# Left tiles with two lodgers: 592 columns of a half-kept weight granule stay in SBUF

## The chip, the cores and the metric

The kernel runs on one core of one Trainium2 chip. The metric is the device time of one execution in microseconds. All durations below come from one profiled execution or from the timed runs of the kernel before.

## What is computed

The reference adds three things: the input `x` [1, 2048, 1024], a recurrent attention layer on the layer-normalised `xn`, and a routed feed-forward for two rows. The attention sets the time. It walks over 64 segments of 32 rows; each segment takes an 8-row memory that is the output of the segment before:

```python
mem = mem0
for s in range(64):
    xs = xn[:, 32*s:32*(s+1), :]
    h = jnp.concatenate([mem, xs], axis=1)            # 8 + 32 rows
    q, k, v = h @ Wq, h @ Wk, h @ Wv                  # 32 heads of 128; each weight 1024 x 4096
    p = softmax(where(mask, q @ k.T * scale, -1e9))
    o = (p @ v) @ Wo                                  # 4096 x 1024
    mem = o[:, :8, :]                                 # needed by the next segment
    outs.append(o[:, 8:, :])
out = x + concatenate(outs) + routed(xn)
```

The routed part picks the two rows of `xn` with the largest score, sends them through a gated feed-forward (three weights of 1024 x 3584) and adds the result at those rows.

## The kernel before

**Rows.** Of a segment's 40 rows, the first 8 outputs feed the next segment's memory. A segment's "main" rows are the memory and the first 24 rows of x (`XM` = 24). The last 8 rows of a segment, the "left" rows, wait for nobody, so those of four segments (a group `G` of segments with `j` = 0, 1, 2, 3) are put together into 32 rows, and their projections are computed once per group: V with segment j = 0 of the group itself, Q with j = 1 and K with j = 2 for the next group. The left queries and keys go to DRAM (`ql_d`, from `XBl`, line 672) and come back a segment at a time (`LX`, line 453).

**Weights.** The four weights are cut into 64 granules of 128 x 2048 (512 KB): granules 0 to 47 are Q, K and V in six phases of eight (`PHASES`), granules 48 to 63 the output projection, counted by `w`. 44 granules are resident in SBUF. The rest is streamed again in each segment from a DRAM copy (`wsc`) through five slots named `g`; `fetch` (line 329) issues one transfer on the SP queue when a slot comes free. Granule 11 (`KEPT_WHOLE`) has its columns in PSUM (`KEPT`), and granule 25 (`KEPT_PART`) has columns 1024 to 2047 there; `kept_piece` (line 349) copies them into the granule's slot in each segment. So 18 granules travel whole, and of granule 25 columns 0 to 1023, 256 KB.

**Order.** The order of each engine's instructions is the order in which the program issues them (`tc.manual_schedule()`); waits on data are added between them. Work that belongs beside the matmuls is hung on a place `(p, kc)`, after granule kc of phase p, by `hook`; `todo` carries hooks into the next segment. In a segment: six phases of eight granules (lines 641 to 657), each with four matmuls, one for each quarter of the columns; scores, exponent and `soften` for two halves of the heads (hooks (2, 6) to (5, 0)); `attend(0, 0)` at (5, 4) and `attend(0, 1)` at (5, 6), `attend(1, ...)` at w = 5 and 8; the output projection, which begins at line 692. The result goes through `mem_to_st` into the next segment's `ST`.

**The tiles of the change.**

- `PL` [128, 4, 2, 32]: the left rows' probabilities. `clear_pl` at (1, 0) sets the columns of the segment before to zero on POOL (line 591), `soften` writes this segment's columns (line 560), and DVE transposes the whole (line 563) into `PTl`.
- `OTL` [128, 4, 8, 32], tag "otl": the left rows' attention outputs of one group. `attend` writes block j (line 587, on ACT and DVE). At j = 3 its columns are projected into `WL` (line 700); the projections of some resident granules are carried into the next segment, up to hook (2, 2), and `store_left` follows at (2, 4). At j = 1, blocks 2 and 3, still free, hold `XBl`, the left queries on their way to DRAM (line 669).
- `XL`, tag "xl" [128, 256]: the x of the left rows. It is loaded by four DMAs on POOL (line 289) twice in a group: at j = 0 for the next group, where `norm_left` normalises it and `new_stl` at w = 13 turns it into `STL`; and at j = 3 for this group at (2, 0), where `sum_left` at (5, 3) makes the residual of it, which starts the accumulation in `WL` at w = 1 (line 738).
- Tag "vl" [128, 1024]: the left rows' V (`VL`), from phase 4 of j = 0 to `attend(1, 1)` of j = 3; then `OL`, the left rows' output.

Of the kernel before, what the change touches and what calls it, by code (L numbers as in the profile page):

```python
# [19 lines left out]
KEPT_WHOLE = 11  # L20
KEPT_PART = 25
LEFT_OUT = 35
NEG = -30000.0

PHASES = [(0, 0), (1, 0), (0, 1), (1, 1), (2, 0), (2, 1)]
# [3 lines left out]
def kernel(  # L29
# [16 lines left out]
    nc = tc.nc  # L46
# [61 lines left out]
    def columns(g, s):  # L108
        if s > 0 and g == KEPT_WHOLE:
            return None  # L110
        return slice(0, 1024 if s > 0 and g == KEPT_PART else 2048)

    wsc = {g: dram.tile([P, columns(g, 1).stop - columns(g, 1).start], BF16, name=f"wsc{g}")
           for g in streamed if g != KEPT_WHOLE}
# [15 lines left out]

    XS = const.tile([P, 256], BF16, name="XS")
    XN = const.tile([P, 256], BF16, name="XN")
    PL = const.tile([P, 4, 2, 32], BF16, name="PL")
    CT = const.tile([P, 32], F32, name="CT")
    MASK = CT[:, 0:12].bitcast(BF16)
    NEGR = CT[:, 13:14]
# [10 lines left out]
    ML = BS[:, 448:448 + 2 * NT].rearrange("p (t c) -> p t c", c=2)  # L147
    nc.vector.memset(SPS[:, :, :, :], 0.0)
    nc.vector.memset(XN[:, :], 0.0)
    nc.gpsimd.memset(PL[:, :, :, :], 0.0)  # L150
    nc.vector.memset(NMSK, 0.0)

    hm = resident[-1]
# [128 lines left out]
        PTm = turn(OB)  # L282
        nc.vector.tensor_copy(out=gview(st)[:, :, :, XM:SEG], in_=PTm[:, :, :, XM:SEG])  # L283

    def load_left(G):
        t = one.tile([P, 256], BF16, tag="xl", name="XL")
        o4 = x2[4 * G * SEG:4 * (G + 1) * SEG, :].rearrange("(s r) d -> s r d", s=4)
        for g in range(4):
            nc.gpsimd.dma_start(out=t[32 * g:32 * (g + 1), :], in_=o4[:, XM:SEG, 256 * g:256 * (g + 1)])
        return t  # L290
# [38 lines left out]
            nc.sync.dma_start(out=t[:, c], in_=wsc[g][:, :])  # L329
        queued.append((g, t))  # L330

    def part(t, jq):
        return t[:, 512 * jq:512 * (jq + 1)]


    def keep(g, t):
        for c, K in KEPT_COLS[g].items():
            turned = PTB.rearrange("p (i r) -> p i r", i=4)
            for i in range(4):
                nc.tensor.transpose(out=turned[:, i, :], in_=t[:, 512 * c + P * i:512 * c + P * (i + 1)],  # L340
                                    identity=IDENT[:, :])
# [49 lines left out]
    XL0 = load_left(0)  # L391
    OB = one.tile([P, 256], BF16, tag="bA", name="MEM0")
    nc.vector.memset(OB[:, :], 0.0)
    for g in range(4):
# [100 lines left out]
    for s in range(NSEG):  # L495
# [53 lines left out]
        def soften(half):  # L549
            S8 = SPS.rearrange("p i a k -> p (i a) k")  # L550
            DN = one.tile([P, 8], F32, tag="nm", name="DN")
            nc.vector.tensor_reduce(out=DN[:, :], in_=S8, axis=AX.X, op=ALU.add)
            nc.vector.reciprocal(out=DN[:, :], in_=DN[:, :])
            PT2 = one.tile([P, 2, 4, 64], BF16, tag=("bA", "bE")[half], name="PT2")
            PTm, PTl = PT2[:, 0], PT2[:, 1]
            PM = PTl.rearrange("p i q -> p (i q)").rearrange("p (b k) -> p b k", b=8)
            PLt = PL.rearrange("p i a k -> p (i a) k")
            dnb = DN[:, :].unsqueeze(2)
            nc.vector.tensor_tensor(out=PM, in0=S8[:, :, 0:32], in1=dnb.to_broadcast([P, 8, 32]), op=ALU.mult)
            nc.vector.tensor_tensor(out=PLt[:, :, XL * j:XL * (j + 1)], in0=S8[:, :, 32:NK],  # L560
                                    in1=dnb.to_broadcast([P, 8, XL]), op=ALU.mult)
            nc.vector.transpose(out=PTm.rearrange("p i q -> p (i q)"), in_=PM.rearrange("p b k -> p (b k)"))
            nc.vector.transpose(out=PTl.rearrange("p i q -> p (i q)"), in_=PLt.rearrange("p b k -> p (b k)"))
            PTs[half] = (PTm, PTl)

        def attend(half, ph):
# [15 lines left out]
            for jl in range(2):  # L582
# [3 lines left out]
                h0 = 16 * half + 8 * ph + 4 * jl  # L586
                copy(out=left_out()[:, j, :, h0:h0 + 4].rearrange("p r i -> p i r"), in_=ov[:, :, SEG:NK])  # L587

        def clear_pl():
            jp = (j + 3) % 4  # L590
            nc.gpsimd.memset(PL.rearrange("p i a k -> p (i a) k")[:, :, XL * jp:XL * (jp + 1)], 0.0)

        def get_left():
            nxt["xl"] = load_left(G if j == 3 else G + 1)

        def prep_left():
            if j == 0:
                norm_left(nxt["xl"], G + 1)
            else:
                sum_left(nxt["xl"], G)  # L600

        for at, fn in todo:
            hook(*at, fn)
        todo = []
        hook(1, 0, clear_pl)
        if s > 0:
            for c in (0, 2, 1, 3):
                hook(0, (1, 3, 1, 3)[c], lambda c=c: kept_piece(KEPT_WHOLE, c, (nc.scalar.copy, nc.vector.tensor_copy)[c // 2]))
# [5 lines left out]
        hook(3, 3 if j == 2 or s == 0 else 0, lambda: soften(0))  # L614
        if s + 1 < NSEG:
            hook(2, 0, lambda: load_seg(s + 1))
        if j == 3 or (j == 0 and G + 1 < NT):
            hook(2 if j else 3, 0, get_left)
            hook(5, 3, prep_left)
        hook(4, 6, lambda: scores(1))  # L620
        hook(5, 0, exponent)
# [1 line left out]
        hook(5, 4, lambda: attend(0, 0))  # L623
        hook(5, 6, lambda: attend(0, 1))

        def left_pass(PSl, g, Gv, first_, last_):
            for jq in range(4):
                nc.tensor.matmul(PSl[32 * jq:32 * jq + 32, :], lhsT=STL[:, g % KC, :], rhs=part(Gv, jq),  # L628
                                 start=first_, stop=last_, tile_position=(0, 32 * jq))

        left_before = False
        for p, (mat, half) in enumerate(PHASES):
# [8 lines left out]
            for kc in range(KC):  # L641
                g = 8 * p + kc
                Gv = granule(g)
                for jq in range(4):
                    nc.tensor.matmul(PSm[32 * jq:32 * jq + 32, :], lhsT=ST[:, kc, :], rhs=part(Gv, jq),  # L645
                                     start=(kc == 0), stop=(kc == KC - 1), tile_position=(0, 32 * jq))
# [12 lines left out]
            if mat < 2:  # L659
# [3 lines left out]

                def store_ql(mat=mat, half=half, PSl=PSl):
                    if mat == 0:
                        XBl = left_out()[:, 2:4].rearrange("p s r h -> p (s r h)")
                    else:
                        XBl = one.tile([P, 512], BF16, tag=("bA", "vl" if s == 0 else "kt")[half], name="XBl")[:, :]
                    nc.scalar.copy(out=XBl, in_=PSl[:, :])
                    if s == 0:  # L670
                        hooks[p + 1, 3].insert(0, lambda m=mat, h=half, b=XBl: turn_first(m, h, b))
                    (nc.gpsimd if s == 0 else nc.scalar).dma_start(out=ql_d[left[mat]][2 * half + mat], in_=XBl)
# [20 lines left out]
        if s + 1 < NSEG:  # L693
            norm_seg(s + 1)

        def project(PS, w, Gv, lhs, last):
            for hs in range(2):
                h = 2 * w + hs
                for g in range(4):
                    nc.tensor.matmul(PS[32 * g:32 * g + 32, 0:256], lhsT=lhs(h),  # L700
                                     rhs=Gv[:, D * hs + 256 * g:D * hs + 256 * (g + 1)], start=False,
                                     stop=(last and hs == 1), tile_position=(0, 32 * g), skip_group_check=True)

        def lhs_main(h):
# [11 lines left out]
        final = (carried or late or [None])[-1]  # L716
        behind = []
        for w in range(16):
            if w == 5:
# [6 lines left out]
            project(WO, w, Gv, lhs_main, w == 15)  # L726
            if j == 3:
                if w in home_w:
                    fn = lambda w=w, Gv=Gv: project(WL, w, Gv, lhs_left, w == final)
                    if w in late:  # L730
                        fill.append(fn)
                    else:
                        todo.append((((1, 2), (1, 4), (1, 7), (2, 1), (2, 2))[len(todo)], fn))
                else:
                    behind.append((w, Gv))
                if w == 1:
                    WL = psL.tile([P, 512], F32, tag="accl", name="WL")
                    nc.tensor.matmul(WL[:, 0:256], lhsT=IDENT[:, :], rhs=nxt["xl"][:, :], start=True, stop=False,
                                     skip_group_check=True)
                if w >= 1:  # L740
                    for w_, Gv_ in behind:
                        project(WL, w_, Gv_, lhs_left, False)
                    behind = []
            if w == 9 and s + 1 < NSEG:
                new_lx(s + 1)
            if w == 10 and s + 1 < NSEG:
                nxt["st"] = new_st(s + 1)
            if w == 13 and j == 0 and G + 1 < NT:
# [32 lines left out]
    for at, fn in todo:  # L781
# [116 lines left out]
```

## Time and profile before

| | |
|---|---|
| Timed runs, us | 1988.77, 1984.77, 1990.33; median 1988.77 |
| The profiled execution, us | 1984.53 |
| Its span, us | 1982.9 |
| Busy share of the span: PE, DVE, ACT, POOL | 82%, 45%, 37%, 22% |
| Granted TensorE clock, mean | 0.957 |
| Moved by DMA | 712.42 MB, mean 359 GB/s |
| `g<-wsc` issues of 512 KB / 256 KB | 1134 / 63 |
| ... median time from issue to landing, us | 6.0 / 5.0 |

The span runs from the first to the last instruction. In the rows of groups, the numbers behind the bar are the group's busy time in us and the mean ns of one; in the list of waits they are the total in us, the count and the longest. In the timeline, the columns are start, duration, engine, line, operation, tiles, and in square brackets the idle time before it and what ended it. A stretch of the table by windows has busy us and the number of instructions for each engine, then the granted clock, the mean busy share of the 16 DMA engines (packets in flight can bring it a little over 1) and GB/s.

### The profile page before, as it was taken

To read this page: it belongs to the slowest core of one execution; us is meant where nothing else is said; L and a number is where in the kernel's file an instruction comes from. 1 tells how busy PE (TensorE), PEld (TensorE's weight loads), DVE (VectorE), ACT (ScalarE), POOL (GpSimd) and SP (SyncE) were. 2 spreads that over 40 slices of the span, in tenths; PEclk is the share of its full clock that TensorE was granted. 3 is DMA by queue.
4 is the path that set the end of the run, shared out by engine and by line. 5 is a ranking of instruction groups with operands and counts; after the bars stand their busy time and mean duration, and the time that the engine had idled before them with its cause. 6 is when DMAs were issued, how large, how long until landed. Compare 5 with 4: busy or idle time off the path is not lost. (4 is left out here: it accounts for less than half of the span.)

```text
span 1982.9 us, 82788 instructions
## 1 busy us (share of the span) xinstructions
PE 1630.3 (82%) x36080; PEld 893.2 (45%) x36080; DVE 883.9 (45%) x2848; ACT 733.5 (37%) x1995; POOL 436.4 (22%) x883
## 2 busy tenths in 40 slices
PE   3468898989888888989888888989888898988863
PEld 1224444444454444445454444545444444544443
DVE  5834444444444434444454444444444444444430
ACT  1124343434334343433444344443434343343330
POOL 3112213112221311222121221222131122212110
PEclk8669999999999999999999999999999999999995
DMA  9999999999999999999999999999999999999998
GB/s 370 403 340 371 353 358 347 366 362 348 375 336 367 366 336 357 360 367 346 372 356 364 356 360 372 350 371 364 361 355 350 355 362 362 333 369 354 353 391 333
DMA packets 232123, 712.42 MB, mean 359 GB/s; under 512 B 39296, under 2 KB 53168, under 8 KB 231760
## 3 DMA queue, kind: packets, MB, share of 16 engines
q1 hardware_dynamic: 194384, 671.18, 90.9%
q0 software_dynamic: 28736, 28.09, 4.4%
q10 hardware_dynamic: 8640, 7.87, 1.2%
q8 instruction: 282, 4.62, 0.9%
q14 instruction: 81, 0.66, 0.1%
HBM read 694.32 MB, written 22.29 MB: 361 GB/s over the span
## 5 line engine op out<-in xcount | busy, mean ns | idle before, releaser
L645 PE MATMUL PSm<-wres,ST 128*32 128x512 bf16 x8448 | 719.3, 386 | 10.7 <-DVE ST L283 5.4
L645 PEld LDWEIGHTS <-ST 128*32 128x32 bf16 x12288 | 327.0, 96 | 439.2 <-issue 219.6
L645 PE MATMUL PSm<-g,ST 128*32 128x512 bf16 x3840 | 392.4, 388 | 125.6 <-DMA g<-wsc 116.0
L700 PE MATMUL WO<-wres,OT 128*32 128x256 bf16 x5632 | 234.2, 280 | 21.4 <-DMA wres<-in_A_Wo_dram 11.4
L700 PEld LDWEIGHTS <-OT 128*32 128x32 bf16 x8192 | 203.9, 98 | 105.5 <-issue 82.3
L661 ACT CAST XB<-PSm 128x512 bf16<-128x512 f32 x256 | 150.5, 588 | 264.1 <-PE PSm L645 264.0
L453 POOL DMA_DIRECT2D LX<-ql_d x63 | 33.6, 534 | 954.4 <-DVE OTL L587 371.7
L628 PE MATMUL PSl<-wres,STL 128*32 128x512 bf16 x2112 | 201.4, 390 | 5.6 <-ACT VL L688 3.7
L349 DVE COPY g<-KEPT 128x512 bf16<-128x512 bf16 x252 | 95.1, 419 | 195.4 <-PE PSm L645 146.1
L763 POOL DMA_DIRECT2D out_dram<-XN x256 | 129.4, 513 | 226.7 <-DVE XN L761 220.9
L253 POOL DMA_DIRECT2D XN<-in_A_x_dram x256 | 128.8, 508 | 205.1 <-PE PSm L645 69.1
L520 DVE COPY KT<-BT 128x512 bf16<-128x512 bf16 x128 | 53.4, 417 | 245.8 <-PE BT L510 203.3
L700 PE MATMUL WO<-g,OT 128*32 128x256 bf16 x2560 | 133.0, 282 | 34.2 <-DMA g<-wsc 23.2
L684 ACT CAST VM<-PSm 128x512 bf16<-128x512 f32 x128 | 79.5, 621 | 107.3 <-PE PSm L645 107.3
L510 PE MATMUL BT<-IDENT,XB 128*128 128x128 bf16 x1024 | 102.3, 223 | 15.9 <-ACT XB L661 14.5
L510 PEld LDWEIGHTS <-XB 128*128 128x128 bf16 x1024 | 58.7, 98 | 121.9 <-ACT XB L661 71.2
L628 PEld LDWEIGHTS <-STL 128*32 128x32 bf16 x3072 | 83.8, 98 | 65.8 <-issue 15.9
L537 DVE TENSOR_TENSOR BS<-BS,CT 128x96 f32<-128x96 f32 (+1 forms) x256 | 59.7, 233 | 106.8 <-PE BS L530 102.3
L515 ACT COPY QT<-BT 128x512 bf16<-128x512 bf16 x128 | 75.2, 588 | 84.0 <-PE BT L510 43.8
L761 DVE CAST XN<-WO 128x128 bf16<-128x128 f32 x64 | 18.7, 292 | 196.0 <-ACT XN L760 196.0
L578 PEld LDWEIGHTS <-VM 32*128 32x128 bf16 x2048 | 69.7, 91 | 75.7 <-issue 71.5
L547 ACT ACTIVATE BS<-BS 128x320 f32<-128x320 f32 x128 | 54.1, 423 | 119.6 <-DVE BS L543 119.5
(161 smaller groups left out, 2413.8 us busy)
## 6 DMA issues: line engine op xcount, KB each, us to landing
g<-wsc SPq DMA_DIRECT2D x1134, 512.0 KB, 6.0
g<-wsc SPq DMA_DIRECT2D x63, 256.0 KB, 5.0
LX<-ql_d POOLq DMA_DIRECT2D x63, 128.0 KB, 6.1
MW<-in_B_w_gate_dram SPq DMA_DIRECT2D x16, 448.0 KB, 9.5
MW<-in_B_w_up_dram SPq DMA_DIRECT2D x16, 448.0 KB, 9.0
wres<-in_A_Wq_dram SPq DMA_DIRECT2D x12, 512.0 KB, 11.5
MW<-in_B_w_down_dram SPq DMA_DIRECT2D x12, 512.0 KB, 10.1
wres<-in_A_Wk_dram SPq DMA_DIRECT2D x11, 512.0 KB, 13.1
```

The lines of the kernel that those rows point to most:

```text
L253: nc.gpsimd.dma_start(out=XN[32 * g:32 * g + XM, :], in_=x2[s * SEG:s * SEG + XM, 256 * g:256 * (g + 1)])
L349: copy(out=t[:, 512 * c:512 * (c + 1)], in_=KEPT_COLS[g][c])
L510: nc.tensor.transpose(out=PTq[:, il, :, :].rearrange("p j r -> p (j r)"), in_=XB[:, il * P:(il + 1) * P], identity=IDENT[:, :])
L515: nc.scalar.copy(out=QT[half][:, :, :], in_=pv)
L537: nc.vector.tensor_tensor(out=S4, in0=S4, in1=m, op=ALU.add)
L578: nc.tensor.matmul(o, lhsT=VM[half][q0:q0 + 32, il * P:(il + 1) * P], rhs=PTm[q0:q0 + 32, il, 0:NK], start=True, stop=False, tile_position ...
L628: nc.tensor.matmul(PSl[32 * jq:32 * jq + 32, :], lhsT=STL[:, g % KC, :], rhs=part(Gv, jq), start=first_, stop=last_, tile_position=(0, 32 ...
L645: nc.tensor.matmul(PSm[32 * jq:32 * jq + 32, :], lhsT=ST[:, kc, :], rhs=part(Gv, jq), start=(kc == 0), stop=(kc == KC - 1), tile_position= ...
L661: nc.scalar.copy(out=XB[:, :], in_=PSm[:, :])
L684: nc.scalar.copy(out=VM[half][:, :], in_=PSm[:, :])
L700: nc.tensor.matmul(PS[32 * g:32 * g + 32, 0:256], lhsT=lhs(h), rhs=Gv[:, D * hs + 256 * g:D * hs + 256 * (g + 1)], start=False, stop=(last ...
L763: nc.gpsimd.dma_start(out=out2[s * SEG:s * SEG + XM, 256 * g:256 * (g + 1)], in_=OB[32 * g:32 * g + XM, :])
```

## The change

- A new tile `HB` [128, 592] holds columns 0 to 591 of granule 25; it is filled once, in segment 0. `columns` gives 592 to 1023 for the transfer in the later segments: 432 columns, 864 B for each partition. `pieces` replaces `part` and gives the matmuls of a quarter their operands: quarter 0 reads `HB`, quarter 1 is two matmuls (80 columns of `HB`, 432 of the slot), quarters 2 and 3 read the slot.
- `PL` is gone. The left probabilities lie in block 3 of `OTL`. At j = 0 the whole block is cleared, at (2, 3), after the last projection of the group before; at j > 0 the columns of the segment before, at (1, 0).
- The tag "xl" is gone. The next group's x (j = 0) is loaded into block 1 of `OTL`; the left queries of j = 1 use blocks 1 and 2. This group's x (j = 3) is loaded into the tag "vl" at w = 9, after `attend(1, 1)`. `sum_left` moves to (0, 6) of the next segment, and the residual is the last matmul into `WL`, at (2, 2), where it was the first.

```diff
+HB_COLS = 592
     def columns(g, s):
...
-        return slice(0, 1024 if s > 0 and g == KEPT_PART else 2048)
+        return slice(HB_COLS, 1024) if s > 0 and g == KEPT_PART else slice(0, 2048)
-    PL = const.tile([P, 4, 2, 32], BF16, name="PL")
+    HB = const.tile([P, HB_COLS], BF16, name="HB")
-    nc.gpsimd.memset(PL[:, :, :, :], 0.0)
-    def load_left(G):
-        t = one.tile([P, 256], BF16, tag="xl", name="XL")
+    def load_left(G, t):
-    def part(t, jq):
-        return t[:, 512 * jq:512 * (jq + 1)]
+    def pieces(s, g, t, jq):
+        c0, c1 = 512 * jq, 512 * (jq + 1)
+        if s == 0 or g != KEPT_PART or c0 >= HB_COLS:
+            return [(0, 512, t[:, c0:c1])]
+        n = min(c1, HB_COLS) - c0
+        return [(0, n, HB[:, c0:c0 + n])] + ([(n, 512, t[:, c0 + n:c1])] if n < 512 else [])
     def keep(g, t):
+        if g == KEPT_PART:
+            nc.vector.tensor_copy(out=HB[:, :], in_=t[:, 0:HB_COLS])
...
-            PLt = PL.rearrange("p i a k -> p (i a) k")
+            PLt = zeros_and_left().rearrange("p r h -> p (r h)").rearrange("p (b k) -> p b k", b=8)
+        def zeros_and_left():
+            return left_out()[:, 3]
         def clear_pl():
-            jp = (j + 3) % 4
-            nc.gpsimd.memset(PL.rearrange("p i a k -> p (i a) k")[:, :, XL * jp:XL * (jp + 1)], 0.0)
+            z = zeros_and_left().rearrange("p r h -> p (r h)")
+            if j:
+                z = z.rearrange("p (b k) -> p b k", b=8)[:, :, XL * (j - 1):XL * j]
+            nc.gpsimd.memset(z, 0.0)
         def get_left():
-            nxt["xl"] = load_left(G if j == 3 else G + 1)
+            nxt["xl"] = load_left(G + 1, left_out()[:, 1].rearrange("p r h -> p (r h)"))
         def prep_left():
-            if j == 0:
-                norm_left(nxt["xl"], G + 1)
-            else:
-                sum_left(nxt["xl"], G)
+            norm_left(nxt["xl"], G + 1)
-        hook(1, 0, clear_pl)
+        hook(*((1, 0) if j else (2, 3)), clear_pl)
-        if j == 3 or (j == 0 and G + 1 < NT):
-            hook(2 if j else 3, 0, get_left)
+        if j == 0 and G + 1 < NT:
+            hook(4 if s == 0 else 3, 0, get_left)
             hook(5, 3, prep_left)
...
-                    nc.tensor.matmul(PSm[32 * jq:32 * jq + 32, :], lhsT=ST[:, kc, :], rhs=part(Gv, jq),
-                                     start=(kc == 0), stop=(kc == KC - 1), tile_position=(0, 32 * jq))
+                    for c0, c1, rhs in pieces(s, g, Gv, jq):
+                        nc.tensor.matmul(PSm[32 * jq:32 * jq + 32, c0:c1], lhsT=ST[:, kc, :], rhs=rhs,
+                                         start=(kc == 0), stop=(kc == KC - 1), tile_position=(0, 32 * jq))
...
-                        XBl = left_out()[:, 2:4].rearrange("p s r h -> p (s r h)")
+                        XBl = left_out()[:, 1:3].rearrange("p s r h -> p (s r h)")
...
                 if w == 1:
                     WL = psL.tile([P, 512], F32, tag="accl", name="WL")
-                    nc.tensor.matmul(WL[:, 0:256], lhsT=IDENT[:, :], rhs=nxt["xl"][:, :], start=True, stop=False,
-                                     skip_group_check=True)
...
+            if w == 9 and j == 3:
+                LR = load_left(G, one.tile([P, 256], BF16, tag="vl", name="XL")[:, :])
...
+            def add_left(WL=WL, LR=LR):
+                nc.tensor.matmul(WL[:, 0:256], lhsT=IDENT[:, :], rhs=LR, start=False, stop=True, skip_group_check=True)
...
-            todo.append(((2, 4), store_left))
+            todo.insert(0, ((0, 6), lambda G=G, LR=LR: sum_left(LR, G)))
+            todo += [((2, 2), add_left), ((2, 4), store_left)]
```

The left pass (`left_pass`) takes its operands from `pieces` in the same way. XL0, the first group's x, is loaded into the tag "vl".

More of the change, by code (lines that the diff above doesn't have):

```diff
@@ L390 @@
     load_seg(0)
-    XL0 = load_left(0)
+    XL0 = load_left(0, one.tile([P, 256], BF16, tag="vl", name="XL0")[:, :])
     OB = one.tile([P, 256], BF16, tag="bA", name="MEM0")
@@ L624, with left_pass @@
         hook(5, 6, lambda: attend(0, 1))
-        def left_pass(PSl, g, Gv, first_, last_):
+        def left_pass(PSl, g, Gv, first_, last_, s=s):
             for jq in range(4):
-                nc.tensor.matmul(PSl[32 * jq:32 * jq + 32, :], lhsT=STL[:, g % KC, :], rhs=part(Gv, jq),
-                                 start=first_, stop=last_, tile_position=(0, 32 * jq))
+                for c0, c1, rhs in pieces(s, g, Gv, jq):
+                    nc.tensor.matmul(PSl[32 * jq:32 * jq + 32, c0:c1], lhsT=STL[:, g % KC, :], rhs=rhs,
+                                     start=first_, stop=last_, tile_position=(0, 32 * jq))
         left_before = False
@@ L644 @@
                 for jq in range(4):
-                    nc.tensor.matmul(PSm[32 * jq:32 * jq + 32, :], lhsT=ST[:, kc, :], rhs=part(Gv, jq),
-                                     start=(kc == 0), stop=(kc == KC - 1), tile_position=(0, 32 * jq))
+                    for c0, c1, rhs in pieces(s, g, Gv, jq):
+                        nc.tensor.matmul(PSm[32 * jq:32 * jq + 32, c0:c1], lhsT=ST[:, kc, :], rhs=rhs,
+                                         start=(kc == 0), stop=(kc == KC - 1), tile_position=(0, 32 * jq))
                 if g in KEPT_COLS and s == 0:
@@ L694, with project @@
             norm_seg(s + 1)
-        def project(PS, w, Gv, lhs, last):
+        def project(PS, w, Gv, lhs, last, first_=False):
             for hs in range(2):
@@ L700, in project @@
                     nc.tensor.matmul(PS[32 * g:32 * g + 32, 0:256], lhsT=lhs(h),
-                                     rhs=Gv[:, D * hs + 256 * g:D * hs + 256 * (g + 1)], start=False,
+                                     rhs=Gv[:, D * hs + 256 * g:D * hs + 256 * (g + 1)], start=(first_ and hs == 0),
                                      stop=(last and hs == 1), tile_position=(0, 32 * g), skip_group_check=True)
@@ L715 @@
         late = home_w[len(carried):]
-        final = (carried or late or [None])[-1]
+        first_left = j == 3
         behind = []
@@ L728 @@
                 if w in home_w:
-                    fn = lambda w=w, Gv=Gv: project(WL, w, Gv, lhs_left, w == final)
+                    fn = lambda w=w, Gv=Gv: project(WL, w, Gv, lhs_left, False)
                     if w in late:
@@ L737 @@
                     WL = psL.tile([P, 512], F32, tag="accl", name="WL")
-                    nc.tensor.matmul(WL[:, 0:256], lhsT=IDENT[:, :], rhs=nxt["xl"][:, :], start=True, stop=False,
-                                     skip_group_check=True)
                 if w >= 1:
                     for w_, Gv_ in behind:
-                        project(WL, w_, Gv_, lhs_left, False)
+                        project(WL, w_, Gv_, lhs_left, False, first_left)
+                        first_left = False
                     behind = []
```

## The prediction

> **What bounds the kernel now.** I read the page's DMA rows first, because the change takes bytes off one weight stream.
>
> ```profile
> DMA packets 232123, 712.42 MB, mean 359 GB/s; under 512 B 39296, under 2 KB 53168, under 8 KB 231760
> q1 hardware_dynamic: 194384, 671.18, 90.9%
> q0 software_dynamic: 28736, 28.09, 4.4%
> q10 hardware_dynamic: 8640, 7.87, 1.2%
> ```
>
> The shares add up to 97.7% with the small queues: the 16 DMA engines are hardly ever idle, and q1, the weight stream, is nearly all of it. Next, the waits: who starves?
>
> ```profile
> PE PSm L645 <- DMA g<-wsc: 116.0, 196, 2.1
> PE WO L700 <- DMA g<-wsc: 23.2, 62, 1.5
> ```
>
> TensorE waits 139 us for streamed granules, some 2.2 us a segment, so a shorter stream finds a taker. But an average over the span hides stages, so I cut four segments in the middle (28 to 30 us each, from one output projection's first matmul at L692 to the next) and asked for busy times by stretch. The first row runs from segment 31 (j = 3, last of its group) into segment 32; the others start at j = 0, 1 and 2.
>
> ```profile
> core 0: us, PE busy (x) PEld busy (x) DVE busy (x) ACT busy (x) POOL busy (x), PEclk, DMA share, GB/s
> 1008.80:1038.30 29.50, 28.01 (x671) 16.51 (x674) 13.11 (x45) 11.53 (x34) 9.47 (x18) 1.00 0.95 348
> 1038.30:1066.00 27.70, 24.61 (x543) 13.03 (x541) 12.72 (x42) 12.27 (x34) 4.77 (x10) 1.00 0.96 359
> 1066.00:1094.00 28.00, 24.31 (x546) 13.10 (x549) 11.84 (x38) 11.20 (x31) 4.70 (x10) 1.00 0.99 372
> 1094.00:1122.00 28.00, 21.52 (x485) 11.74 (x481) 13.30 (x47) 10.85 (x31) 7.04 (x14) 1.00 0.99 370
> ```
>
> Three stretches of four leave PE 3 to 6 us idle while DMA is at 0.96 to 0.99: they are bound by transfers. The first is another matter: PE is busy 28.0 of 29.5 us (the left rows' output projection and V pass lie there) and DMA is the one with slack, 0.95. Bytes saved pay in three segments of four; a delay of PE at j = 3 costs.
>
> **Part 1, the shorter transfer (gain).** Granule 25 loses 592 of its 1024 streamed columns: 592 x 2 B x 128 = 151,552 B in each of 63 segments, 9.55 MB. By q1's own row that is 9.55 / 671.18 x 90.9% of 1982.9 us = 25.6 us, the upper end. But one packet goes to each partition, and a shorter packet is dearer by the byte. The trace's packet records, by size, have medians of 27 ns (512 B), 46 (1024), 84 (2048) and 159 (4096): 9 ns plus 0.0366 ns per byte. The new 864 B row then takes 41 ns in place of 84: 43 ns x 128 / 16 engines = 0.344 us a segment, 21.7 us over 63. The lower end takes 53 ns, the mean of a 1024 B packet on q0: (84 - 53) x 8 x 63 = 15.6 us. I take 21.7: the line goes through all four sizes.
>
> The packet records fit a cost by packet and byte. The Trainium skill's "DMA: Bandwidth & Descriptors" (section "How a descriptor splits into AXI transactions") speaks against this length: a descriptor that doesn't start on a 256 B boundary also fetches the bytes below it, and rows of 864 B start at such a boundary one time in eight; by an estimate from its 32 B beats, 3.5 more a row at some 1.2 ns, it would take 2 us off the gain. No row of this trace shows such a length. The same page (section "Where 436 GB/s comes from") has some 358 GB/s per core as the HBM limit, by which the gain would be 9.55 MB / 358 GB/s = 26.7 us; the trace speaks against it as a cap, since 1002.65 to 1008.80 us moved 420 GB/s.
>
> Where does it land? 48 of the 63 transfers lie in stretches bound by DMA: 48 x 0.344 = 16.5 us. The other 15 belong to a j = 0 segment, in the stretch that PE nearly fills; I count half, 15 x 0.17 = 2.6 us. **Gain: 19 us**, bounds 14 to 25.6.
>
> **Part 2, the probabilities' new place (cost).** PL had a tile of its own; now the left probabilities lie in row block 3 of OTL. At j = 3 the attention outputs go into that very block, so the first OTL copy on ACT must wait until DVE has transposed the second half's probabilities. The timelines of ACT and DVE at the end of segment 31 put a number on it:
>
> ```profile
> 1007.06 0.27 ACT L585 CAST OT<-WO 128x128 bf16<-128x128 f32 x1 [1.60 <-PE BT L580]
> 1007.22 0.31 ACT L587 CAST OTL<-WO 128x32 bf16<-128x32 f32 x1
> 1007.30 0.34 ACT L585 CAST OT<-BT 128x128 bf16<-128x128 f32 x1
> 1007.52 0.32 ACT L587 CAST OTL<-BT 128x32 bf16<-128x32 f32 x1
> ```
>
> ```profile
> 1007.19 0.45 DVE L563 STREAM_TRANSPOSE PT<-PL 128x256 bf16<-128x256 bf16 x1
> ```
>
> The copy that started at 1007.22 could now start at 1007.64, 0.42 later. Over the 16 segments with j = 3 the same difference (end of that transpose less the start of the first L587) runs from none to 1.1 us, mean 0.7 over the positive ones and zeros. Queued behind it on ACT are the other OT and OTL copies of that half and VM[1]; PE's second attend group waits for them, because it writes the same PSUM columns, and L692 follows one granule later. So PE starts the stage it is the bound of 0.7 us late. Some of it is swallowed by the few DMA waits there; I let 0.5 us through: **8 us**, bounds 0 and 16 x 2.1 = 34 us, where 2.1 us is what the same difference reads in most j = 2 segments, which run at PE's pace.
>
> **Part 3, small moves.** At j = 1 the query rows leave from blocks 1 and 2 of OTL, and the first OTL copy there must wait for that store's landing. The trace has the landing between 1.2 us before and 0.7 us after the copy's start, 0.15 us late on average; PE waits for DMA there anyway: 0, at most 2 us. Granule 25's second quarter becomes two matmuls (80 and 432 columns); the columns streamed are the same, so only a weight load is new, 96 ns in the row of L645, 63 + 15 times; idle PE covers most, 15 lie in the full stretch: 1 us, bounds 0 and 7.5. At j = 0 POOL clears 256 columns after XN's four loads instead of 64 before them: 0.30 us by the first PL memset against 0.17; queued behind are OL's stores, the XL loads and LX; the first probabilities are written at L560 some 5 us after the last left projection that the memset waits for. Nothing; without that cover 16 x 0.3 = 5 us.
>
> The left x for the residual now loads at w = 9 of j = 3, four POOL issues of 0.59 us behind LX. POOL idles 2.66 us there before the output stores (1012.95 + 0.54 + 2.34 = 1015.8 against 1016.15), so the stores hold their place, at most 1 us late; the next XN load waits for them, 6 us on. Its five DVE operations (1.05 us) move from before the projection to (0, 6) of the next segment. XL lands 5.6 us after issue, near 1021; the copies of granule 25's kept columns queue behind the sum on DVE and are needed only in phase 3, about 1029. The add on PE at (2, 2), near 1024, has some 2 us of cover; if it is gone, PE stalls what is missing, 16 x 0.5 = 8 us at worst. The identity matmul itself only changes place within the same stretch. In the tail, store_left comes some 2.5 us later, and the routed rows behind it; PE finishes the gate matmuls at 1966 and the last weights land at 1976.8: no cost. At the start, one extra DVE copy and a shorter weight copy on POOL: nothing.
>
> **Sum:** -19 + 8 + 1 = -10 us. The profiled execution took 1984.5 us (span 1982.9), so 1974.5 by it; the three runs' median is 1988.8, 4.2 us above, so in the median's terms about 1978.
>
> **Rivals.**
> (a) *All hidden, the full gain.* The j = 3 wait moves PE by less than the DMA waits around it, and the saved bytes pay everywhere: -20 to -25.6 us, 1963 to 1969. For: DMA at 97.7%. Against: the first row of the stretches. 0.20.
> (b) *The gain is eaten.* Packets cost nearer the lower end (-14) and the j = 3 wait goes through whole (16 x 0.7 = 11): -3 us, 1986. For: an unseen packet length; PE at 28.0 of 29.5. 0.21.
> (c) *Slower: the j = 3 wait grows to PE's pace.* With fewer waits for DMA ahead of it, PE reaches the first attend sooner while DVE's chain from scores to transposes keeps its length, so the difference rises towards the 2.1 us of j = 2: 34 us of waiting against 19 gained and 1 lost, +16, near 2004. It decides from about 1.1 us a segment, where 16 x 1.1 = 18 us eats the gain. Against: at j = 3 no transfer before that point gets more than 0.344 us shorter. 0.18.
> (d) *It doesn't do what it says:* the kept columns are simply not fetched, so q1 must shrink by 9.55 MB; only a stall of the whole stream could hide it. Included in (b).
>
> **How the numbers follow.** The forecast has 0.41. A measurement of this kernel can tell about 0.3%, 6 us, from no change. Faster: forecast and (a), 0.61. Same: (b), 0.21. Slower: (c), 0.18. The range, 1962 to 1994, takes in (a) down to the bytes' price, the forecast, (b) and the mild part of (c); the forecast's own range is 1970 to 1983.
>
> **What would show it.** Right: q1 near 661.6 MB; the 256 KB issue group gone and one of 108 KB in its place; DMA waits of PE smaller; in j = 3 an ACT wait "OTL <- DVE PT" of 0.4 to 1 us, 16 times, and L692 later by as much; the j = 3 stretch no shorter, the other three shorter by about 0.35 us. Wrong: packets of 864 B above 53 ns, a j = 3 stretch longer by over 1 us, PE waiting at the moved add, or the DMA share falling without the time.

## The result and the profile after

The changed kernel is slower: 2006.81 us median of 19 runs against 1989.46 of 19 runs of the kernel before, ratio 1.0091, 95% interval 1.0070 to 1.0112. The prediction was 1978, 10 us faster. All ratios below are to the kernel before on the same chip, with the 95% interval in parentheses.

The page of the changed kernel, DMA rows, and its issue rows (KB each, median us to landing):

```profile
DMA packets 232094, 702.75 MB, mean 350 GB/s; under 512 B 39297, under 2 KB 61233, under 8 KB 231729
q1 hardware_dynamic: 194384, 661.63, 90.4%
g<-wsc SPq DMA_DIRECT2D x1134, 512.0 KB, 5.8
g<-wsc SPq DMA_DIRECT2D x63, 108.0 KB, 4.6
```

The bytes went as announced: q1 carries 9.55 MB less, and the 108 KB group is there. But q1's busy time did not fall. 90.4% of a span of 2007.7 us is 1815.0 us of the 16 engines; before it was 90.9% of 1982.9, 1802.5 us. Fewer bytes took longer, so the packets that stayed got dearer. The packet records of q1 between the ninth and the last but one projection start show which. The column with 160 to 180 ns is called the band below:

```
4096 B packets          mean ns   share of 160 to 180 ns   short packets of granule 25, median / mean ns
before                   174.7          4.5%               2048 B: 84 / 102
after                    178.7         12.5%                864 B: 40 / 46
```

The short packet costs about what the line through the sizes gave (41 ns; its median is 40). The 4096 B packets, 2304 a segment, cost 4.0 ns more: 4.0 x 2304 / 16 = 0.58 us a segment, against (102 - 46) x 8 = 0.45 us saved.

The waits after (total us, count, longest):

```profile
PE PSm L656 <- DMA g<-wsc: 111.6, 188, 2.2
DVE XL L303 <- DMA XL<-in_A_x_dram: 56.3, 16, 4.5
PE WO L711 <- DMA g<-wsc: 25.6, 60, 1.7
PE WO L584 <- ACT OTL L593: 16.3, 19, 1.8
PE PSl L638 <- ACT VL L699: 13.4, 14, 2.8
ACT OTL L593 <- DVE PT L569: 12.8, 13, 1.7
```

The kernel before has, at the places of the fourth and fifth of these lines:

```profile
PE WO L578 <- ACT OTL L587: 2.2, 5, 0.7
PE PSl L628 <- ACT VL L688: 3.7, 5, 1.3
```

PE's waits for DMA hardly moved: 137 us against 139. ACT's OTL copy now waits for DVE, 12.8 us in 13 waits, which the kernel before doesn't have, and PE's second attend group (`WO L584`) waits for that copy, 16.3 us against 2.2. The waits for the loaded XL and for the VL copy grew too (e8 below prices them). The timelines of ACT and DVE at the end of segment 31 (line 593 is before's 587, 569 is 563) show one:

```profile
1019.28 0.27 ACT L591 CAST OT<-WO 128x128 bf16<-128x128 f32 x1 [1.11 <-PE BT L586]
1020.44 0.30 ACT L593 CAST OTL<-WO 128x32 bf16<-128x32 f32 x1 [0.89 <-DVE PT L569]
1020.52 0.32 ACT L591 CAST OT<-BT 128x128 bf16<-128x128 f32 x1
```

```profile
1019.91 0.45 DVE L569 STREAM_TRANSPOSE PT<-OTL 128x256 bf16<-128x256 bf16 x1
```

The first OTL copy, which used to follow its OT copy by 0.16 us, now starts 1.16 us after it, just behind the transpose's end (1020.36). The four stretches that answer to those shown before:

```profile
1021.96:1052.16 30.20, 28.44 (x667) 16.97 (x667) 13.65 (x48) 11.35 (x33) 12.00 (x22) 0.95 0.95 330
1052.16:1079.56 27.40, 24.29 (x541) 12.85 (x541) 12.39 (x41) 12.41 (x35) 4.76 (x10) 1.00 0.99 355
1079.56:1107.26 27.70, 25.38 (x539) 13.47 (x539) 11.76 (x38) 11.03 (x32) 4.70 (x10) 0.94 1.01 364
1107.26:1134.82 27.56, 21.64 (x474) 11.41 (x474) 13.02 (x45) 10.90 (x32) 4.71 (x10) 0.99 1.01 386
```

This one group has its loss in the first stretch (30.2 against 29.5 us) and the others 0.3 to 0.4 us shorter, as forecast; over 54 segments the means by j = 3, 0, 1, 2 went from 29.8, 27.8, 28.1, 27.9 to 30.2, 28.2, 28.1, 28.2. So on the whole the other stretches gave nothing: one group is no sample.

### The profile page after: what moved, and what is told of

The parts are those of the page before. It is cut to its first block, busy times and chain, and to the rows that moved or that the text cites. A ratio compares the mean times of both kernels' runs of the same rounds, so it can differ in the third digit from the quotient of the medians.

```text
span 2007.7 us, 83006 instructions
## 1 busy us (share of the span) xinstructions
PE 1647.8 (82%) x36158; PEld 897.8 (45%) x36158; DVE 881.5 (44%) x2849; ACT 735.2 (37%) x1995; POOL 438.8 (22%) x882
## 3 DMA queue, kind: packets, MB, share of 16 engines
q1 hardware_dynamic: 194384, 661.63, 90.4%
## 5 line engine op out<-in xcount | busy, mean ns | idle before, releaser
L656 PE MATMUL PSm<-g,ST 128*32 128x512 bf16 (+1 forms) x3777 | 389.5, 389 | 127.2 <-DMA g<-wsc 111.6
L711 PEld LDWEIGHTS <-OT 128*32 128x32 bf16 x8192 | 209.4, 100 | 101.9 <-issue 74.8
L711 PE MATMUL WO<-wres,OT 128*32 128x256 bf16 x5632 | 242.3, 289 | 12.2 <-DMA wres<-in_A_Wo_dram 10.2
L521 ACT COPY QT<-BT 128x512 bf16<-128x512 bf16 x128 | 75.2, 588 | 90.9 <-PE BT L516 50.4
L584 PEld LDWEIGHTS <-VM 32*128 32x128 bf16 x2048 | 70.0, 92 | 78.9 <-issue 73.5
L638 PE MATMUL PSl<-g,STL 128*32 128x512 bf16 (+1 forms) x945 | 98.4, 392 | 0.0
## 6 DMA issues: line engine op xcount, KB each, us to landing
wres<-in_A_Wk_dram SPq DMA_DIRECT2D x11, 512.0 KB, 12.8
```

The source lines that it names most:

```text
L521: nc.scalar.copy(out=QT[half][:, :, :], in_=pv)
L584: nc.tensor.matmul(o, lhsT=VM[half][q0:q0 + 32, il * P:(il + 1) * P], rhs=PTm[q0:q0 + 32, il, 0:NK], start=True, stop=False, tile_position ...
L638: nc.tensor.matmul(PSl[32 * jq:32 * jq + 32, c0:c1], lhsT=STL[:, g % KC, :], rhs=rhs, start=first_, stop=last_, tile_position=(0, 32 * jq))
L656: nc.tensor.matmul(PSm[32 * jq:32 * jq + 32, c0:c1], lhsT=ST[:, kc, :], rhs=rhs, start=(kc == 0), stop=(kc == KC - 1), tile_position=(0, 3 ...
```

## Experiments

What could make the same 4096 B transfers dearer? In the two programs' layouts two things moved with HB. In SBUF the five slots lie behind the small constant tiles; HB (1184 B) in PL's place (512 B) pushed them by 672 B, from a multiple of 512 B to 160 B past a multiple of 256. In DRAM the copies behind granule 25 moved up. So there were theory A (slots' place in SBUF), B (DRAM) and C (the new waits). In the diffs, "..." marks lines that are left out.

**e1_pad160**: the kernel before, slots pushed to the changed kernel's place within 256 B.

```diff
+    PAD = const.tile([P, 80], BF16, name="PAD")
+    nc.vector.memset(PAD[:, :], 0.0)
```

> The kernel before with 160 unused bytes per partition ahead of the five weight slots, so that these start at 160 past a multiple of 256 B, as in the changed kernel, instead of at a multiple of 512 B; nothing else moves but the small tiles behind them. Theory A (the slots' place in SBUF makes the streamed packets dearer): the 4096 B packets go from a mean of 174.7 ns to about 178.7, 0.56 us of DMA time a segment, so 1.5 to 2% slower (about 2020 to 2028 us beside 1989), with the 160 to 180 ns part of the packets grown as in the changed kernel. Theory B (the place of the weight copies in DRAM, which moved too): no change, within 0.3%. Theory C (the new waits of the left tiles, at j = 3 above all): no change.

Measured 1.0074 (1.0045 to 1.0103), +15 us; 4096 B packets at 177.1 ns, 19.1% of them between 160 and 180. The page's q1 row, beside the before's 90.9% of 1982.9 us with the same packets and bytes, has 91.5% of 1997.1 us: 25 us more busy time.

```profile
q1 hardware_dynamic: 194384, 671.18, 91.5%
```

The direction is A's, the size half. The small tiles behind the slots moved too, but the copies into them kept their time (XB on ACT 587 ns in the mean against 588). How the dearer packets make the kernel longer is not shown in full: PE's waits for `g<-wsc` grew by 4 us (143 against 139), the span by 14.

**e10_pad64**: the same with 64 B (the diff is against e1).

```diff
-    PAD = const.tile([P, 80], BF16, name="PAD")
+    PAD = const.tile([P, 32], BF16, name="PAD")
```

> The kernel before with 64 unused bytes per partition ahead of the slots in place of the 160 that cost 0.74%: the slots start 64 past a multiple of 512 B. If what costs is a start that is no multiple of 64 B: no change (within 0.3%), and the share of 4096 B packets between 160 and 180 ns stays at 4 to 5%. If any start off a multiple of 256 B (or 512) costs: 0.5 to 0.9% slower, that share near 19%.

1.0110 (1.0072 to 1.0147), 24.2% of the packets in the band, mean 176.8. A multiple of 64 B is not enough. Kernels whose slots start at a multiple of 512 B have 3.5 to 4.9% there. The Trainium skill's "DMA: Bandwidth & Descriptors", section "How a descriptor splits into AXI transactions", says of a descriptor that doesn't start on 256 B that bytes ahead of its start are fetched too and cost beats. These runs agree with it only in that a start off 256 B costs: it is a write into SBUF that moved here, the median stays at 159 ns, and 64 B put more packets into the band than 160. No run here tried an odd multiple of 256.

**e3_dram**: the kernel before with the DRAM copies moved within 64 KB as in the change.

```diff
-    wsc = {g: dram.tile([P, columns(g, 1).stop - columns(g, 1).start], BF16, name=f"wsc{g}")
+    wsc = {g: dram.tile([P + 22 * (g == KEPT_PART), columns(g, 1).stop - columns(g, 1).start], BF16, name=f"wsc{g}")[0:P, :]
```

> The kernel before with 22 unused rows (45,056 B) behind the DRAM copy of granule 25, which puts the copies of granules 29 to 62 at the same place within 64 KB as in the changed kernel; SBUF is as before. Theory A: no change, within 0.3%. Theory B: 1.5 to 2% slower, mean of the 4096 B packets about 178.7 ns. Theory C: no change.

0.9999 (0.9963 to 1.0034). B falls.

**e2_hb_behind**: the changed kernel, slots back at a multiple of 512 B.

```diff
-    HB = const.tile([P, HB_COLS], BF16, name="HB")
+    HB = one.tile([P, HB_COLS], BF16, tag="hb", name="HB")
```

> The changed kernel with one thing moved: HB lies behind the five slots instead of ahead of them, so the slots start at a multiple of 512 B again; its DRAM layout, waits and transfers are the changed kernel's. Theory A: the 4096 B packets return to about 175 ns, the shorter transfer pays 0.45 us a segment, less what the waits at j = 3 cost: 0.5 to 1.3% faster than the kernel before (about 1963 to 1979 us). Theory B: as slow as the changed kernel, ratio 1.009. Theory C: ratio 1.009 too.

1.0073 (1.0042 to 1.0104); the band is back at 4.0%, the time is not, and the mean of the 4096 B packets is 177.9 ns, not 175: 3.2 of the 4.0 ns don't come from the slots' place. A alone doesn't explain the result; against the changed kernel's 1.0091 the slots' place is worth 0.2%, which the intervals don't resolve.

**e4_lodging**: the change without HB.

```diff
-HB_COLS = 592
+HB_COLS = 0
...
-    HB = const.tile([P, HB_COLS], BF16, name="HB")
...
-        if g == KEPT_PART:
-            nc.vector.tensor_copy(out=HB[:, :], in_=t[:, 0:HB_COLS])
```

> The changed kernel without HB: the left tiles are shared as in the change, but granule 25 travels with 1024 columns as before, and the slots start at a multiple of 512 B as before. It is the lodging alone. Theory A: what the new waits cost and no more, 0 to 0.6% slower (the prediction's 8 us is 0.4%). Theory B: the same. Theory C: the waits are what made the changed kernel slow: it lost 18 us in spite of 22 us of DMA time saved, so 1.5 to 2% slower here, with the j = 3 stretch longer by some 2 us.

1.0085 (1.0057 to 1.0113): more than the waits' allowance, less than C wanted. The lodging was then halved.

**e8_xl_only**: PL back in its own tile and no HB; the left x lodged as in the change (the diff is against the change).

```diff
...
-            PLt = zeros_and_left().rearrange("p r h -> p (r h)").rearrange("p (b k) -> p b k", b=8)
+            PLt = PL.rearrange("p i a k -> p (i a) k")
...
-        hook(*((1, 0) if j else (2, 3)), clear_pl)
+        hook(1, 0, clear_pl)
```

> The kernel before with one half of the lodging: the left x lies in OTL and in the tag vl, is loaded at w = 9 of j = 3, and sum and add come in the next segment; PL keeps its own tile, granule 25 its 1024 columns, the slots their place. The lodging as a whole cost 0.85%. Theory X (the late sum is the cost: DVE waits for XL's landing, OL leaves later, and VL, which takes OL's tile, holds up PE in phase 5; the loads meet the output projection's traffic): 0.5 to 0.9% slower, with PE waiting on the VL copy some 10 us. Theory P (the first OTL copy at j = 3 is the cost): 0 to 0.3%.

0.9994 (0.9964 to 1.0023): no cost that can be measured, though DVE waits 37 us for XL and PE 9.2 us for the VL copy (3.7 before). Theory X falls.

**e9_pl_only**: the other half, in the kernel before.

```diff
-    PL = const.tile([P, 4, 2, 32], BF16, name="PL")
+    PAD = const.tile([P, 256], BF16, name="PAD")
...
-            PLt = PL.rearrange("p i a k -> p (i a) k")
+            PLt = zeros_and_left().rearrange("p r h -> p (r h)").rearrange("p (b k) -> p b k", b=8)
...
-                        XBl = left_out()[:, 2:4].rearrange("p s r h -> p (s r h)")
+                        XBl = left_out()[:, 1:3].rearrange("p s r h -> p (s r h)")
```

> The kernel before with the other half: the left probabilities lie in block 3 of OTL and the left queries in blocks 1 and 2; XL keeps its tile and its times, and an unused 512 B tile in PL's place keeps the slots where they were. Theory X: 0 to 0.3% slower. Theory P: 0.5 to 0.9% slower, PE waiting at the output projection's start on ACT's OTL copies some 20 us more, all at j = 3, 1.2 us a time.

1.0067 (1.0038 to 1.0097), 13 us. Its waits:

```profile
PE WO L578 <- ACT OTL L587: 14.8, 18, 2.0
ACT OTL L587 <- DVE PT L563: 11.0, 11, 1.9
```

PE loses 12.6 us more at this place than before (2.2), less than the 20 expected and about the whole 13 us. The loss lies where the wait lies, at the end of the stretch that begins at j = 2: its mean goes from 27.9 to 28.6 us, the other three stay within 0.1.

**e13_pl_j3own**: e9, but at j = 3 the probabilities go to the unused tile.

```diff
-            PLt = zeros_and_left().rearrange("p r h -> p (r h)").rearrange("p (b k) -> p b k", b=8)
+            PLt = (PAD[:, :] if j == 3 else zeros_and_left().rearrange("p r h -> p (r h)")).rearrange("p (b k) -> p b k", b=8)
```

> The kernel with the probabilities in OTL (0.67% slower), but at j = 3 they are written into the 512 B tile that lay unused in PL's place; so ACT's first OTL copy at j = 3 no longer waits for DVE, and everything else of that kernel stays. If that wait is the cost: within 0.3% of before. If the cleared block at j = 0 or the wait for the left queries' store at j = 1 is: 0.5 to 0.8% slower still.

1.0014 (0.9987 to 1.0040). ACT's wait for DVE is gone from the list, and PE's wait is down:

```profile
PE WO L578 <- ACT OTL L587: 4.7, 10, 0.7
```

The wait at j = 3 is the lodging's cost; the cleared block at j = 0 and the left queries' move cost nothing that can be measured.

**e5_short**: the transfer alone. `pieces` is the change's, on the kernel before, with granule 24 in HB's place.

```diff
+HB_COLS = 592
...
-        return slice(0, 1024 if s > 0 and g == KEPT_PART else 2048)
+        return slice(HB_COLS, 1024) if s > 0 and g == KEPT_PART else slice(0, 2048)
...
+        return [(0, n, res_tiles[24][:, c0:c0 + n])] + ([(n, 512, t[:, c0 + n:c1])] if n < 512 else [])
```

> The kernel before with the shorter transfer alone: granule 25 travels with columns 592 to 1023, and its columns 0 to 591 are read from resident granule 24 (other weights, the same reads), so there is no HB, no shared left tile, and the slots stay where they were. Quarter 1 is split as in the change. Theory D (the 16 DMA engines' busy time is the bound, as predicted): 0.344 to 0.45 us a segment, 1.1 to 1.4% faster, about 1961 to 1967 us beside 1988. Theory S (five slots and the time from issue to landing set the pace; the granule's slot is held as long whatever it carries): 0 to 0.4% faster, with the other packets growing longer by what the short one saves.

0.9943 (0.9915 to 0.9971), 11 us faster: half of what D asks for at the least (1.1%, 22 us). Short packets fell to 47 ns in the mean, and the 4096 B ones rose to 176.5 with slots where they were.

**e6_none**: no transfer of granule 25; all its streamed columns are read from granule 24.

```diff
...
-        if s > 0 and g == KEPT_WHOLE:
+        if s > 0 and g in (KEPT_WHOLE, KEPT_PART):
             return None
...
```

> As the one before, but granule 25 is not fetched at all after segment 0 (its columns 0 to 1023 are read from resident granule 24; no quarter is split; it still takes a slot). Theory D: the 2048 B packets cost 0.82 us of DMA time a segment, so 2.3 to 2.6% faster, about 1937 to 1943 us. Theory S: less than 1.2% faster, since a slot without a transfer is a slot less to fetch ahead with.

0.9968 (0.9940 to 0.9996). Nearly twice the DMA time is taken away (0.82 us a segment against 0.44) and no more is gained. PE's waits for the stream, in this order those of e5 and of e6:

```profile
PE PSm L652 <- DMA g<-wsc: 94.8, 163, 1.9
PE WO L707 <- DMA g<-wsc: 26.3, 62, 1.4
```

```profile
PE PSm L652 <- DMA g<-wsc: 93.2, 166, 2.8
PE WO L707 <- DMA g<-wsc: 25.6, 63, 1.8
```

The first saving takes 18 us off the before's 139; the second takes off 2. D falls.

**e11_noslot**: e6 without the slot and the kept copies.

```diff
...
-    flow += [(s, g) for s in range(NSEG) for g in streamed]
+    flow += [(s, g) for s in range(NSEG) for g in streamed if s == 0 or g != KEPT_PART]
...
```

> Granule 25 is neither fetched nor given a slot after segment 0 and its kept columns aren't copied; PE reads all of it from resident granule 24 (other weights). Beside the kernel without its transfer (0.9968), it tells what the held slot is worth. Theory S (slots and time to landing set the pace): clearly faster than that kernel, 1.5% or more below before (under 1958 us), since fetching runs a granule further ahead. Theory D' (half of every byte saved comes back as longer packets, and slots don't matter): the same 0.3 to 1% below before, 1966 to 1980 us.

0.9921 (0.9894 to 0.9949), 1969 us. The time lies in the range of D', and S's 1.5% is not reached. But it is 0.5% below e6, with intervals that just overlap, where D' has the slot at nothing: the held slot, with two DVE copies a segment, may be worth that much. Most of the bytes' price stays unpaid even so, and the 4096 B packets are at 178.0 ns.

**e12_hb320**: e8 with 320 columns of HB behind the slots (the diff is against e8).

```diff
-HB_COLS = 0
+HB_COLS = 320
...
+    HB = one.tile([P, HB_COLS], BF16, tag="hb", name="HB")
```

> What the runs point to as a version without the two costs: the left x shares tiles as in the change (free by itself), the probabilities keep their own tile PL (no new wait at j = 3), HB has 320 columns and lies behind the slots, which stay at a multiple of 512 B; granule 25 travels with 704 columns. If the costs are the slots' place and the wait at j = 3: 0.2 to 0.5% faster than before, 320/592 of the 0.57% that the short transfer alone gave. If reading HB beside the slot or the splitting costs something of its own: no change or slower.

1.0000 (0.9966 to 1.0034). The 0.3% hoped for lies inside the interval; inconclusive.

**e14_short_lodged**: does the transfer's gain survive the lodging? The change with granule 24 for HB.

```diff
-    HB = const.tile([P, HB_COLS], BF16, name="HB")
...
-        return [(0, n, HB[:, c0:c0 + n])] + ([(n, 512, t[:, c0 + n:c1])] if n < 512 else [])
+        return [(0, n, res_tiles[24][:, c0:c0 + n])] + ([(n, 512, t[:, c0 + n:c1])] if n < 512 else [])
...
```

> The changed kernel without the tile HB: granule 25 travels with 432 columns and its columns 0 to 591 are read from resident granule 24 (other weights); the left tiles are shared as in the change; the slots start at a multiple of 512 B. If the parts add up (short transfer -0.57%, lodging +0.6 to +0.85%): 0 to 0.3% slower than before. If the short transfer pays nothing once the lodging has made PE late: 0.6 to 0.9% slower, as the changed kernel with HB behind the slots (1.0073).

1.0081 (1.0051 to 1.0110). It doesn't. Its waits at j = 3:

```profile
PE WO L581 <- ACT OTL L590: 18.9, 24, 1.9
ACT OTL L590 <- DVE PT L566: 14.2, 13, 1.8
```

**e15_short_j3own**: the same without the wait at j = 3 (the diff is against e14).

```diff
+    PL3 = const.tile([P, 256], BF16, name="PL3")
...
-            PLt = zeros_and_left().rearrange("p r h -> p (r h)").rearrange("p (b k) -> p b k", b=8)
+            PLt = (PL3[:, :] if j == 3 else zeros_and_left().rearrange("p r h -> p (r h)")).rearrange("p (b k) -> p b k", b=8)
```

> The same, with a 512 B tile of their own for the probabilities at j = 3, so that ACT's first OTL copy there does not wait. If the wait at j = 3 is what eats the short transfer's gain: 0.4 to 0.7% faster than before, as the short transfer alone. If not: as the one before.

0.9960 (0.9924 to 0.9995): 24 us of 1985 between the two, from this one wait. ACT's line is gone from the list of e15, and PE's is down by 14.9 us:

```profile
PE WO L583 <- ACT OTL L592: 4.0, 8, 0.7
```

**e16_short_pad160**: e5 with e1's 160 B.

```diff
+    PAD = const.tile([P, 80], BF16, name="PAD")
```

> The short transfer alone (columns 0 to 591 of granule 25 read from resident granule 24), with the 160 unused bytes ahead of the slots. If the slots' place and the short transfer add up: -0.57% + 0.74%, 0 to 0.4% slower than before, the share of 4096 B packets between 160 and 180 ns near 19%.

1.0028 (0.9999 to 1.0057), 15.2% in the band where 19 was expected. These two add up (-0.57 + 0.74 = 0.17%, well inside the interval).

**e17_both_mended**: e2, and at j = 3 the first half's left outputs wait in a tile of 256 B, paid for with 128 columns of HB (the diff is against e2).

```diff
-HB_COLS = 592
+HB_COLS = 464
...
+    X3 = one.tile([P, XL, 16], BF16, tag="x3", name="X3")
...
-                copy(out=left_out()[:, j, :, h0:h0 + 4].rearrange("p r i -> p i r"), in_=ov[:, :, SEG:NK])
+                to = X3 if j == 3 and half == 0 else left_out()[:, j]
+                copy(out=to[:, :, h0:h0 + 4].rearrange("p r i -> p i r"), in_=ov[:, :, SEG:NK])
+            if j == 3 and half == 0 and ph == 1:
+                nc.vector.tensor_copy(out=left_out()[:, 3, :, 0:16], in_=X3[:, :, :])
```

> The change with both costs mended, in the same SBUF: HB lies behind the slots, which start at a multiple of 512 B, and gives up 128 of its 592 columns (granule 25 travels with 560) for a 256 B tile X3; at j = 3 the first half's left outputs go to X3, so that ACT needn't wait for the transpose of the probabilities, and one DVE copy of 128 columns (about 0.3 us, 16 times) brings them to OTL. If slots' place and wait at j = 3 are the two costs: 0.2 to 0.6% faster than before, about as the short transfer with the wait removed (0.996). If HB itself (its reads, its place) costs: no change.

0.9963 (0.9937 to 0.9989): 1978.4 us against 1987.2 beside it, faster than both kernels, as expected. Its list has no wait of ACT's OTL copy for DVE, and at the place in question:

```profile
PE WO L585 <- ACT OTL L595: 3.2, 8, 0.8
```

## Why the prediction was wrong, point by point

The table has the ratios of the runs by what each kernel has. The transfer of 108 KB is that of 432 columns (with HB, or granule 24 in HB's place). In the rows "at 512" the slots start at a multiple of 512 B, in the rows "shifted" 160 B past a multiple of 256:

| | no new wait at j = 3 | new wait at j = 3 |
|---|---|---|
| 256 KB transfer, at 512 | 1 (before), 0.9994 (e8), 1.0014 (e13) | 1.0067 (e9), 1.0085 (e4) |
| 256 KB transfer, shifted | 1.0074 (e1) | no run |
| 108 KB transfer, at 512 | 0.9943 (e5), 0.9960 (e15) | 1.0073 (e2), 1.0081 (e14) |
| 108 KB transfer, shifted | 1.0028 (e16) | 1.0091 (the change) |

**The step that failed: the wait at j = 3 was let through at 0.5 of 0.7 us and added to the gain as if the two were independent.** The wait itself was the right mechanism: 0.7 us forecast at each of 16 places, 12.8 us in 13 waits found. Alone it cost 13 us (e9) in place of 8, all that PE waits more; by the prediction's own words few DMA waits lie there, so there was little to swallow the rest. With the shorter transfer it cost 24 us (e14 against e15), so nothing is left of the gain: the right-hand column has no run below 1.0067.

**Part 1: the price was right, the place wrong.** The packet costs 40 ns, as worked out. But "48 of the 63 transfers lie in stretches bound by DMA" took a full busy share for a bound by bytes. The transfer alone gave 11 us, not 19; without any transfer it was 6 us (e6). Part of what is missing shows as longer packets, and the held slot may be another part (e11).

**A term was missing: where the slots land.** The change was read as edits of operations. HB was costed for what it saves, and its place, 672 B more ahead of the slots that nearly all traffic writes to, was not in the sum. Without the wait it costs 0.74% (e1) or 0.85% (e16 against e5), 15 to 17 us. In the changed kernel, beside the wait, it can't be told from nothing (1.0091 against 1.0073, e2). The Trainium skill's rule on starts off 256 B ("DMA: Bandwidth & Descriptors", section "How a descriptor splits into AXI transactions") was weighed for the 864 B rows, where by an estimate it was to cost 4 ns (41 to 45 ns); the median in the trace after is 40. What the runs show off 256 B is dearer 4096 B packets; that this is the same rule is not shown.

**The parts don't add up freely.** Alone they are worth -0.57 (e5), +0.67 (e9), +0.74 (e1) and -0.06% (e8), which makes +0.78%, near the 0.91 measured. That is luck: by the table each part's worth depends on the others. Shown is that removing the wait brings the gain back (e15), and that mending both the wait and the slots' place makes the change pay (e17).

**The granted clock is lower where the wait is.** Over each kernel's runs its mean is 0.942 to 0.947 in the five kernels with the wait (the change, e2, e4, e9, e14) and 0.949 to 0.954 in all others. The profiled executions show where: in the first 5 us of the output projection at j = 3, just behind the wait, it is 1.00 in the kernel before, 0.89 to 1.00 in the others without the wait, and 0.74 to 0.89 in the five with it. In the runs of the kernel before, 0.01 less clock goes with some 7 us more time, so by an estimate some 7 of the 24 us between e14 and e15 (0.942 and 0.952) may come with the clock. How much of the wait's cost really goes this way is not shown, and that e9's 13 us equal what PE waits more may be in part chance.

**Part 3 held.** The moved load, sum and add and the clearing at j = 0 cost nothing measurable (e8, e13), although DVE waits 56 us for XL, which I had not forecast: it comes up to 4.5 us late at (0, 6). The cover of the kept copies held.

Among the rivals, (c) has the number nearest to the result, 2004 against 2007, and the right direction, but in part by luck: its wait was to grow towards 2.1 us each and 34 us in all. It grew little, from 11.0 us on ACT in e9 to 14.2 in e14, and the gain was 11 us, not 19. Rival (b) had the wait going through whole and a smaller gain, which is what e9 and e5 show, but its sum of -3 lacked the slots and took the parts as independent. Rival (d) fell with the q1 row.

## What to carry to other kernels

A wait put in front of a stage that one engine fills cost no less than its length here, and it took the gain of another part with it; so run the parts of a change one by one and also each without the other. When a change adds or resizes a tile, list the addresses of every DMA destination behind it: without the wait, 160 B ahead of the stream's buffers cost more (0.74%) than the shorter transfer saved (0.57%). A DMA busy share near full did not mean here that bytes were what is short (e6); take the bytes away once without the rest of the change.

## What was not expected of the hardware

- The start of a 512 KB transfer's SBUF rows matters: 64 or 160 B past a multiple of 256 put 24 or 19% of the 4096 B packets between 160 and 180 ns, against 4.5% at a multiple of 512, with the same median of 159 ns; 1.1 and 0.7% of the kernel's time (e10, e1).
- q1's busy share stayed between 90.1 and 91.5% in all kernels, with 654.66 to 671.18 MB moved. The packets that stay get longer as others go: the mean of the 4096 B packets went from 174.7 ns to 178.0 as granule 25 left the stream (e11).
- A wait of 0.8 us in the mean ahead of the output projection (PE's, 14.8 us in 18 waits in e9) goes with a lower granted clock behind it: 0.74 over the projection's first 5 us at j = 3 in e9 and 0.78 in the changed kernel, 1.00 in the kernel before.
